# Gates and values of pairs of 512-token blocks by seven products in place of eight, with the weights' combinations formed on the chip and held in DRAM

## The chip, the cores and the metric

The kernel runs on one core of one Trainium2 chip. The metric is the device time of one execution, in microseconds (us), as the median of several runs. The kernel before has a median of 1006.23 us over 3 runs (1005.33 to 1008.88).

## The reference, cut to what matters

Attention on 8 batches of 576 tokens with 8 heads of 64, half of the heads with a local mask of 32 keys and half with a strided one, and then a gated layer on all 4608 tokens:

```python
scores = scale * np.matmul(q, k.transpose(0, 1, 3, 2))
...
attn_out = np.matmul(attn, v)                      # (8, 8, 576, 64)
x = attn_out.transpose(0, 2, 1, 3).reshape(4608, 512)
gate = 1.0 / (1.0 + np.exp(-(x @ w_gate)))         # w_gate: 512 x 1536
val = x @ w_val                                    # w_val:  512 x 1536
out = (gate * val) @ w_out                         # w_out: 1536 x 512
```

The output is 4608 x 512 in float32.

## The kernel before

**Tiling.** The tokens go in nine blocks of 512: block b below 8 holds the first 512 tokens of batch b, and block 8 holds the 64 tokens left over of each batch. The 1536 columns of the gated layer go in 12 slices f of 128. For a slice of a block TensorE forms the gates (`glu_gate`, L371) and the values (`glu_val`, L388), 128 columns by 512 tokens each, in `products` (L364), and a step later adds the slice's share of the output into four PSUM banks (`glu_out`, L416). Each float32 factor is kept as a rounded float32r part h and a rest l, and a product is three matmuls: h by h, h by l and l by h. So the gates of a slice take 4 chunks of the 512 inner columns by 3 matmuls, 12; the values 12; the outputs 4 groups of 128 tokens by 3, 12. A slice is 36 matmuls of 128x128 by 512 columns, a block is 432, and nine blocks are 3888.

**Weights.** The weights come as 64-bit words. In the first stretch of the program they are loaded 512 KB at a time (`load_weight`, W in the order below), turned into float32 by ScalarE (a, b) and VectorE (w), and split into h (u, ScalarE) and l (l, GpSimd). They then stay in SBUF until the end.

**Attention.** A batch has four steps (`pair`, L164), each for two heads: loads (Q, V), scores on TensorE (S), mask, maximum and difference on VectorE (F), exponential on ScalarE (E), sum and division on VectorE (N), a transposition, weighing of the values on TensorE (X), and the split of the result into h (H, ScalarE) and l (L, VectorE), with the left-over tokens set aside (R). The transposition is on TensorE with a copy by ScalarE (T, P) for batches below `BY_PE`, and else in eight pieces on VectorE (B, `turn_blocks`, L254).

**Order.** The first stretch (batches 0 and 1, block 0 and all weights) is written out by hand in `ORDER`, L58, a list of short names that every engine follows. From block 1 on, only TensorE's order is written by hand (L515 to L526): per slice gates, values, outputs of the slice before, and at two of every nine places the next piece of attention(k + 1). A scheduler orders the other engines. DMAs are issued by SyncE (SP), which takes its list in order and waits at an entry until that entry may go.

Of the kernel before, what the change touches and what calls it, by code (L numbers as in the profile page):

```python
# [53 lines left out]

ORDER = """  # L58
C Q00 Q01 W0.0 S00 Z00 F00 S01 a0.0 Q03 W0.1 Q02 b0.0 Z01 F01 E00 W1.0 V01 V00 N00 E01 a0.1 N01 T00 b0.1 W1.1
P00 w0.0 S02 a1.0 b1.0 w0.1 T01 u0.0 W0.2 Z02 F02 u0.1 l0.0 X00 P01 l0.1 a1.1 w1.0 E02 S03 V02 N02 R00 H00  # L60
a0.2 b1.1 L00 T02 b0.2 W2.0 w1.1 u1.0 W2.1 X01 P02 l1.0 Z03 F03 u1.1 g0.0.0 V03 l1.1 Q10 g1.0.0 R01 H01 g0.1.0
w0.2 g1.1.0 E03 L01 a2.1 N03 u0.2 g1.0.1 b2.1 l0.2 X02 a2.0 b2.0 w2.1 W1.2 W2.2 g0.0.1 V10 w2.0 H02 T03 R02
u2.1 L02 g1.1.1 P03 l2.1 g1.0.2 u2.0 a1.2 X03 l2.0 b1.2 W3.0 w1.2 g1.1.2 H03 g0.0.2 R03 L03 u1.2 g0.1.1 a2.2
l1.2 g1.1.3 b2.2 g0.0.3 a3.0 W3.1 w2.2 g0.1.2 s0 g1.0.3 g0.1.3 u2.2 g2.0 b3.0 m0 l2.2 a3.1 W3.2 w3.0 s1 u3.0
b3.1 l3.0 g2.1 x0 W4.0 w3.1 a3.2 y0 u3.1 m1 S10 b3.2 l3.1 x1 W4.1 w3.2 O0 Q11 s2 y1 u3.2 Z10 F10 a4.0 l3.2
b4.0 g3.0 a4.1 W4.2 w4.0 b4.1 E10 W5.0 w4.1 O1 m2 u4.1 N10 x2 l4.1 s3 g3.1 y2 a4.2 u4.0 T10 m3 b4.2 l4.0 g4.1
x3 W5.1 w4.2 P10 y3 a5.0 u4.2 g4.0 b5.0 l4.2 W5.2 w5.0 a5.1 b5.1 u5.0 W6.0 w5.1 X10 s4 l5.0 u5.1 m4 O2 V11
l5.1 a5.2 R10 b5.2 a6.0 W6.1 w5.2 H10 g5.1 b6.0 L10 u5.2 W6.2 w6.0 x4 l5.2 u6.0 y4 O3 a6.1 l6.0 b6.1 W7.0 w6.1
a6.2 g5.0 b6.2 u6.1 W7.1 w6.2 l6.1 u6.2 O4 a7.0 l6.2 s5 b7.0 m5 a7.1 W7.2 w7.0 x5 S11 b7.1 y5 g6.0 u7.0 W8.0
w7.1 Q12 l7.0 Z11 F11 u7.1 a7.2 l7.1 b7.2 g6.1 s6 W8.1 w7.2 a8.0 E11 g7.0 m6 u7.2 N11 x6 l7.2 a8.1 g7.1 s7 y6  # L70
b8.0 T11 m7 b8.1 W8.2 O5 w8.0 P11 W9.0 w8.1 u8.0 l8.0 u8.1 X11 x7 l8.1 a8.2 y7 O6 V12 a9.0 b8.2 b9.0 W9.1 w8.2
R11 g8.0 W9.2 w9.0 u8.2 H11 l8.2 u9.0 L11 g8.1 s8 l9.0 a9.1 b9.1 a9.2 W10.0 w9.1 O7 b9.2 m8 u9.1 W10.1 w9.2 x8
l9.1 y8 u9.2 S12 a10.0 l9.2 b10.0 g9.1 Z12 F12 Q13 W10.2 a10.1 b10.1 W11.0 w10.1 E12 g9.0 w10.0 u10.1 N12
u10.0 l10.1 O8 a10.2 s9 l10.0 T12 b10.2 m9 g10.0 P12 W11.1 w10.2 x9 u10.2 y9 l10.2 X12 s10 a11.0 g10.1 V13 R12
H12 b11.0 L12 W11.2 w11.0 S13 m10 u11.0 O9 Z13 F13 l11.0 x10 a11.1 b11.1 y10 g11.0 E13 w11.1 u11.1 N13 O10 s11
l11.1 a11.2 T13 b11.2 g11.1 P13 w11.2 u11.2 l11.2 X13 m11 x11 R13 y11 H13 L13
# [7 lines left out]
def attention_then_glu(ctx, tc, qk_l, qk_s, v_l, v_s, w_all, consts, out):  # L84
    nc = tc.nc
    pool = ctx.enter_context(tc.tile_pool(name="keep", bufs=1))
    work = ctx.enter_context(tc.tile_pool(name="work", bufs=1))
# [21 lines left out]
    wh, wl = {}, {}

    def stage(n, name):
        return work.tile([P, DM if n[0] in "hl" else 2 * DM], I32, tag=n, name=name)

    def weight_tiles(f):
        wh[f], wl[f] = [None] * 3, [None] * 3
        for i in range(3):
            w = pool.tile([P, 2, DM], F32R, name=f"w{f}_{i}")
            wh[f][i], wl[f][i] = w[:, 0], w[:, 1]

    raws, words = {}, {}  # L120

    order = [(0, 0), (0, 1), (1, 0), (1, 1), (0, 2), (2, 0), (2, 1), (1, 2), (2, 2)]
    order += [(f, i) for f in range(3, NF) for i in range(3)]

    def load_weight(f, i):

        at = order.index((f, i)) % 2
        raws[f, i] = stage(f"raw{at}", f"raw{f}_{i}").rearrange("p (n t) -> p n t", t=2)
        nc.sync.dma_start(raws[f, i], w_all[f, :, i, :, :])

    def upper_words(f, i):
        n = order.index((f, i))
        at = 0 if f == LATE else n % 3
        words[f, i] = stage(f"h{at}", f"high{f}_{i}"), stage(f"l{at}", f"low{f}_{i}")

        to, word = words[f, i][0].bitcast(F32), raws[f, i][:, :, 1].bitcast(F32)
        nc.scalar.activation(to, word, AF.Prelu, scale=2.0**-112, alpha=2.0**32)  # L139

    def lower_words(f, i):
        word = raws.pop((f, i))[:, :, 0].bitcast(U32)
        nc.scalar.activation(words[f, i][1], word, AF.Copy, scale=2.0**-29)  # L143

    def whole(f, i):

        high, low = words[f, i]
        nc.vector.tensor_scalar(high, high, 3, None, op0=ALU.logical_shift_left)
        nc.vector.tensor_tensor(high, high, low, op=ALU.add)  # L149

    def upper(f, i):
        if f == LATE and i == 2:
            w = stage("raw0", f"w{f}_{i}").bitcast(F32R)
            wh[f].append(w[:, :DM]), wl[f].append(w[:, DM:])
        elif f == LATE:
            for ws, t in ((wh, "h"), (wl, "l")):
                ws.setdefault(f, []).append(stage(f"{t}{i + 1}", f"{t}{f}_{i}").bitcast(F32R))
        nc.scalar.copy(wh[f][i], words[f, i][0].bitcast(F32))  # L158

    def lower(f, i):  # L160
        a, _ = words.pop((f, i))
        nc.gpsimd.tensor_tensor(wl[f][i], a.bitcast(F32), wh[f][i].bitcast(F32), op=ALU.subtract)  # L162

    def pair(b, step, space):  # L164
# [5 lines left out]
        nv = (VL if local else SS) * P  # L170
        tiles = {}

        def load_qk(queue=nc.sync):
# [1 line left out]
            queue.dma_start(qk[:, :cols], (qk_l if local else qk_s)[b, p])
# [236 lines left out]
    def glu_out(k, f):  # L416
# [13 lines left out]
        if f < NF - 1:  # L430
            return
# [178 lines left out]
```

## Time and profile before

| | |
|---|---|
| median of 3 runs (lowest, highest) | 1006.23 us (1005.33, 1008.88) |
| the profiled execution: span from the first to the last instruction | 1008.5 us |
| granted TensorE clock in it, mean | 0.998 |
| DMA traffic in it | 66.02 MB |
| HBM read and written | 55.42 MB and 9.44 MB |

The profile gives no time of its own for the execution beside the span, so the span is what a sum is made against. PE is the row of matmuls, PEld that of TensorE's weight loads, DVE is VectorE, ACT ScalarE, POOL GpSimd. Matmuls overlap: the listed duration of one is longer than the distance from one to the next, and the distance is read from merged pieces of the chain of waits ("x12" is twelve matmuls in a row). Idle time of an engine that others do not wait for costs nothing.

### The profile page before, as it was taken

How to read it: one execution, taken by the hardware profiler on the slowest of the kernel's cores; microseconds unless marked ns; L12 is line 12 of the kernel's file. 1: busy time of each engine (PE TensorE's matmuls, PEld its weight loads, DVE VectorE, ACT ScalarE, POOL GpSimd, SP SyncE). 2: the span in 40 equal slices, each digit the busy share in tenths (PEclk: the TensorE clock that was granted, in tenths of full speed). 3: DMA queues.
4: the chain of work that ended last, by engine and by line, in shares of the span. 5: the costliest groups of instructions: out<-in, count | busy, mean ns of one | idle time of the engine just before them, and what ended most of it. 6: DMA issues, size and time to landing. Idle time of an engine off the chain costs nothing.

```text
span 1008.5 us, 18125 instructions
## 1 busy us (share of the span) xinstructions
PE 976.4 (97%) x7840; PEld 793.5 (79%) x7840; DVE 584.4 (58%) x1006; ACT 323.8 (32%) x637; POOL 53.7 (5%) x56
## 2 busy tenths in 40 slices
PE   4899998999999999999999999999999999999997
PEld 3687776888888888888888888888888888888885
DVE  6787766666666566666666666656665733333322
ACT  4787763222322222222222232222222322222221
POOL 1343320000000000000000000000000000000000
PEclk9999999999999999999999999999999999999999
DMA  7665632111211111111111121112110010001001
GB/s 265 210 190 185 202 99 93 40 52 41 83 51 52 41 51 61 49 42 48 71 41 52 41 93 42 52 41 72 62 52 17 1 43 1 0 1 42 1 1 42
DMA packets 19872, 66.02 MB, mean 65 GB/s; under 512 B 2257, under 2 KB 2385, under 8 KB 19793
## 3 DMA queue, kind: packets, MB, share of 16 engines
q1 hardware_dynamic: 18352, 59.28, 18.1%
q10 hardware_dynamic: 1440, 5.59, 1.6%
q8 instruction: 61, 1.00, 0.4%
q14 instruction: 19, 0.15, 0.0%
HBM read 55.42 MB, written 9.44 MB: 64 GB/s over the span
## 4 chain that ended last, share of the span: by engine, by line
PE 85%; DMA 6%; DVE 4%; ACT 4%; issue 0%; SPq 0%; ACTq 0%; DVEq 0%
PE o L423 27%; PE v L369 26%; PE g L369 26%; DMA raw<-in_w_all 5%; PE x L289 3%; PE s L208 2%; ACT high L139 1%; ACT low L143 1%; DVE sb L228 1%; DVE sb L239 0%; DVE high L149 0%; DVE mx L227 0%; DMA qk<-in_qk_l 0%; DVE pt L261 0%; DVE mx L236 0%
## 5 line engine op out<-in xcount | busy, mean ns | idle before, releaser
L423 PE MATMUL o<-w,hh 128*128 128x512 f32 x864 | 270.7, 394 | 1.2 <-DVE ob L436 1.2
L369 PE MATMUL g<-xh,w 128*128 128x512 f32 x784 | 259.3, 391 | 3.8 <-ACT e L378 2.3
L369 PE MATMUL v<-xh,w 128*128 128x512 f32 x784 | 261.4, 394 | 1.1 <-POOL w L162 0.9
L423 PEld LDWEIGHTS o<-w,hh 128*128 128x128 f32 x864 | 159.4, 188 | 36.4 <-issue 2.0
L369 PEld LDWEIGHTS g<-xh,w 128*128 128x128 f32 x784 | 147.4, 188 | 35.6 <-ACT e L378 3.2
L369 PEld LDWEIGHTS v<-xh,w 128*128 128x128 f32 x784 | 147.2, 188 | 34.1 <-POOL w L162 1.4
L423 PE MATMUL o<-w,hl 128*128 128x512 f32 x432 | 168.6, 390 | 0.0
L386 DVE TENSOR_SCALAR t<-t 128x512 int32<-128x512 int32 x96 | 41.0, 427 | 217.9 <-ACT t L383 217.2
L369 PE MATMUL g<-xl,w 128*128 128x512 f32 x392 | 153.0, 390 | 0.4 <-DVE xl L324 0.4
L369 PE MATMUL v<-xl,w 128*128 128x512 f32 x392 | 153.1, 390 | 0.0
L402 ACT ACTIVATE hh<-t 128x512 fp32r<-128x512 f32 x108 | 68.2, 632 | 257.5 <-DVE t L411 255.3
L383 ACT ACTIVATE t<-g 128x512 f32<-128x512 f32 x96 | 57.4, 598 | 267.0 <-PE g L369 262.7
L410 DVE SCALAR_TENSOR_TENSOR e<-e,v 128x512 f32<-128x512 f32 x96 | 65.8, 685 | 91.1 <-PE v L369 91.1
L405 DVE SCALAR_TENSOR_TENSOR hl<-t,hh 128x512 fp32r<-128x512 f32 x108 | 76.7, 710 | 51.1 <-ACT hh L402 51.0
L261 DVE STREAM_TRANSPOSE pt<-sb 32x320 f32<-32x320 f32 (+1 forms) x192 | 103.0, 536 | 3.1
L423 PEld LDWEIGHTS o<-w,hl 128*128 128x128 f32 x432 | 81.1, 188 | 17.9 <-DVE hl L405 0.6
L369 PEld LDWEIGHTS g<-xl,w 128*128 128x128 f32 x392 | 73.7, 188 | 15.8 <-DVE xl L324 0.7
L369 PEld LDWEIGHTS v<-xl,w 128*128 128x128 f32 x392 | 73.6, 188 | 14.4
L411 DVE SCALAR_TENSOR_TENSOR t<-t,e 128x512 f32<-128x512 f32 x96 | 66.5, 692 | 3.2
L384 ACT ACTIVATE e<-g 128x512 f32<-128x512 f32 x96 | 57.0, 594 | 0.0
L162 POOL TENSOR_TENSOR w<-high,w 128x512 fp32r<-128x512 f32 x34 | 46.2, 1369 | 93.6 <-ACT w L158 93.6
L289 PEld LDWEIGHTS x<-pt,vv 64*64 64x64 f32 (+1 forms) x1856 | 34.4, 139 | 12.0 <-issue 10.4
(61 smaller groups left out, 675.6 us busy)
## 6 DMA issues: line engine op xcount, KB each, us to landing
raw<-in_w_all SPq DMA_DIRECT2D x36, 512.0 KB, 4.3
qk<-in_qk_s SPq DMA_DIRECT2D x14, 599.0 KB, 4.1
vv<-in_v_l SPq DMA_DIRECT2D x13, 640.0 KB, 3.9
qk<-in_qk_l SPq DMA_DIRECT2D x14, 592.0 KB, 4.0
out<-ob SPq DMA_DIRECT2D x32, 256.0 KB, 2.0
vv<-in_v_s SPq DMA_DIRECT2D x13, 384.0 KB, 3.0
vv<-in_v_l ACTq DMA_DIRECT2D x3, 640.0 KB, 3.8
qk<-in_qk_s ACTq DMA_DIRECT2D x2, 599.0 KB, 5.2
```

The lines of the kernel that those rows point to most:

```text
L162: nc.gpsimd.tensor_tensor(wl[f][i], a.bitcast(F32), wh[f][i].bitcast(F32), op=ALU.subtract)
L261: nc.vector.transpose(dst[to : to + LB, :, col : col + LB], src[rows : rows + LB, :, h * LB : (h + 1) * LB])
L289: nc.tensor.matmul(xp[j * D : (j + 1) * D, r * BANK + (u * per + g) * m : r * BANK + (u * per + g + 1) * m], v[rows, (u * per + g) * P + j ...
L369: nc.tensor.matmul(o, w, x, start=first and n == 0, stop=last and n == len(todo) - 1)
L383: nc.scalar.activation(t, g, AF.Tanh, scale=0.5)
L384: nc.scalar.activation(e, g, AF.Exp)
L386: nc.vector.tensor_scalar(ti, ti, 0x7FFFFFFF, None, op0=ALU.bitwise_and)
L402: nc.scalar.activation(hh, t, AF.Copy, scale=half)
L405: nc.vector.scalar_tensor_tensor(hl, t, half, hh.bitcast(F32), op0=ALU.mult, op1=ALU.subtract)
L410: nc.vector.scalar_tensor_tensor(e, e, 1.0, v, op0=ALU.min, op1=ALU.mult)
L411: nc.vector.scalar_tensor_tensor(t, t, 1.0, e, op0=ALU.add, op1=ALU.mult)
L423: nc.tensor.matmul(acc[k][i], h[:, i * P : (i + 1) * P], w, start=f == 0 and n == 0, stop=f == NF - 1 and n == 2,)
```

## The change

Blocks 1 to 8 are taken two at a time: (1, 2), (3, 4), (5, 6) and (7, left-over). For such a pair, and for two slices f at a time, gates and values are 2x2 block products: the inner 512 columns in two halves by the two slices, against the same halves by the two blocks. One level of Strassen's scheme (in Winograd's form) forms them from seven products of half the inner length instead of eight: P1 to P7, each 2 chunks by 3 matmuls, for gates and for values. That is 7 x 6 x 2 = 84 matmuls for two slices of two blocks, where there were 4 x 24 = 96.

**The sums.** Seven combinations of x per pair of blocks are formed by VectorE and split by ScalarE and VectorE (`mix_input`, written J in the order; T are the four differences, h and l the splits). Seven combinations of the weights per two slices are formed by GpSimd from the float32 weights and split, 1792 KB for gates and as much for values, once, in the first pair of blocks; they are used from SBUF there, stored in DRAM, and loaded again for the other three pairs (`load_mix`). The sums of products are made in PSUM: ScalarE copies a bank onto another or into SBUF and the next product is added onto it (`pair_of_chunks`). The gate is a Sigmoid on ScalarE, where it was a Tanh and an Exp with three VectorE operations behind them.

**The outputs** of a pair of blocks come after all its gates and values: eight groups of three slices (`group_of_outs`, 36 matmuls each), whose split weights were stored in DRAM in the first stretch and are loaded again for every group, 1536 KB each (`load_outs`). The split of gate times value is made at that load. Loads go into a ring of four tiles w0 to w3, two for each stage, and `load` of a stage is written ahead of the stage before it.

**Elsewhere.** Batch 2 is now in the hand-written order too (`BY_PE` is 3, so it is transposed on TensorE), `ORDER` is new, and the left-over tokens go through DRAM (`rests`). The pieces of attention are placed in the pair stages by a clock that counts products: S at 1, 13, 25 and so on, X at 10.5 after the start, 22.5 and so on.

```diff
-BY_PE = 2
-AT = (0, 7)
-LATE = NF - 1
+BY_PE = 3
...
+PIECE_0, PIECE, PIECE_X = 1, 12, 9.5
+SUPER = ((1, 2), (3, 4), (5, 6), (7, None))
+W_OF = dict(P1=0, P2=1, P4=2, P5=3, P6=4, P7=5, P3=6)
+X_OF = dict(P1=0, P5=1, P2=2, P6=3, P3=4, P7=5, P4=6)
...
+H22 JT1 R22 T23 Jh1 P23 Jl1 X23 H23 JT2 R23 Jh4 JT3 Jh3 Jl4 Jh5 Jl3 Jl5 JT4 Jh6 Jl6
...
+    def keep_rests(b):
+        nc.sync.dma_start(rests[b], rest[b])
...
     def lower(f, i):
...
+        if i == 2:
+            g, n = divmod(f, THREE)
+            nc.sync.dma_start(outer[g][:, n * 2 * DM : (n + 1) * 2 * DM], t.bitcast(F32))
...
+    OBS = ("ob0", "ob1", "ob0", "ob1")
...
+    def next_of_ring(name, n):
+        tag = f"w{ring[0] % 4}"
+        ring[0] += 1
+        return flat(tag, n, name, F32R)
+
+    def load_mix(s, p, i):
+        t = next_of_ring(f"mix{s + 1}_{p}_{i}", 2 * MIX)
+        hold["mix", i, p] = t
+        if s:
+            nc.sync.dma_start(t.bitcast(F32), mixed[p, i])
+            return
...
+        st = flat("st", 4 * PART, f"sums{p}_{i}")
+        s1, s2, s3, s4 = (st[:, n * PART : (n + 1) * PART] for n in range(4))
+        tt = nc.gpsimd.tensor_tensor
+        tt(s1, a21, a22, op=ALU.add)
+        tt(s2, s1, a11, op=ALU.subtract)
+        tt(s3, a11, a21, op=ALU.subtract)
+        tt(s4, a12, s2, op=ALU.subtract)
+        at = 0
+        for src in (a1, a22, st):
+            n = src.shape[1]
+            nc.scalar.copy(t[:, at : at + n], src)
+            tt(t[:, MIX + at : MIX + at + n], src, t[:, at : at + n].bitcast(F32), op=ALU.subtract)
+            at += n
+        nc.sync.dma_start(mixed[p, i], t.bitcast(F32))
...
+        run("P1", g1, v1, lambda: nc.scalar.copy(g2, g1), lambda: nc.scalar.copy(v2, v1))
+        run("P5", g5, v5, lambda: nc.scalar.copy(new("gp"), g5), lambda: nc.scalar.copy(new("vp"), v5))
+        run("P6", g2, v2, lambda: nc.scalar.copy(new("gq"), g2), lambda: nc.scalar.copy(new("vq"), v2), False)
+        run("P2", g1, v1, lambda: sig(new("s11"), g1), lambda: mul(h1[:, :TB], tmp["s11"], v1), False)
...
+        run("P7", g2, v2, *sums("p", "22", g2, v2), False)
+        with tc.high_priority():
+            mul(h2[:, TB:], tmp["s22"], tmp["v22"])
+        run("P3", g5, v5, *sums("q", "12", g5, v5), False)
+        with tc.high_priority():
+            mul(h1[:, TB:], tmp["s12"], tmp["v12"])
+        run("P4", g2, v2, lambda: sig(new("s21"), g2), lambda: mul(h2[:, :TB], tmp["s21"], v2), False)
+
+    def load_outs(s, n):
+        j, g = divmod(n, GROUPS // 2)
...
+        nc.sync.dma_start(hold["o"][-1].bitcast(F32), outer[g])
+        for q in range(THREE):
+            src = hs[g * THREE + q][:, j * TB : (j + 1) * TB]
+            hh, hl = (hold["h"][-1][:, (2 * q + k) * TB : (2 * q + k + 1) * TB] for k in range(2))
+            nc.scalar.copy(hh, src)
+            nc.vector.tensor_tensor(hl, src, hh.bitcast(F32), op=ALU.subtract)
+
+    def group_of_outs(s, n, banks, tick):
+        j, g = divmod(n, GROUPS // 2)
+        (g1, g2, g5), (v1, v2, v5) = banks
+        accs = ([g1, v1, g5, v5], [g1, v1, g2, v2])[j]
...
+        if g == GROUPS // 2 - 1:
+            b = SUPER[s][j]
+            last = s == len(SUPER) - 1 and j
+            with tc.high_priority():
+                store(accs, b, ("ob0", "ob1", "t0", "t1") if last else OBS)
...
+            if k + 1 < len(stages):
+                load(*stages[k + 1])
+            (pair_of_chunks if kind == "p" else group_of_outs)(s, n, banks, tick)
```

**Three places in the order.** The first is VectorE where block 0 ends. Before, ob_1 and ob_3 (two of the four copies of block 0's output) stand among the work on block 1; sb_0 and pt_0 are the first attention step of batch 2, e, t and hl belong to block 1's slices 0 and 1:

```order
L410 SCALAR_TENSOR_TENSOR e_0_1787<-e_0_1787,v_0_1859 128x512
L239 TENSOR_TENSOR sb_0_1799<-sb_0_1799,mx_0_1800 128x640
L411 SCALAR_TENSOR_TENSOR t_0_1788<-t_0_1788,e_0_1787 128x512
L261 STREAM_TRANSPOSE pt_0_1850<-sb_0_1799 32x10x32 x8
L436 COPY ob_1_1893<-o_0_748 128x512
L405 SCALAR_TENSOR_TENSOR hl_0_1873<-t_0_1788,hh_0_1872 128x512
L386 TENSOR_SCALAR t_1_1916<-t_1_1916 128x512
L436 COPY ob_3_1899<-o_1_749 128x512
```

Now the same two copies stand ahead of the last attention step of batch 2 (first_x_103 is its probabilities, s_3 its scores), and the differences and splits of x for the first pair of blocks follow (raw_396 is batch 1, raw_1290 batch 2):

```order
L448 COPY ob_1_1876<-o_0_666 128x512
L448 COPY ob_3_1882<-o_1_667 128x512
L207 TENSOR_TENSOR first_x_103<-s_3_1836,cst 128x6x54 x2
L208 TENSOR_REDUCE first_x_104<-first_x_103 128x12
L209 TENSOR_TENSOR first_x_103<-first_x_103,first_x_104 128x12x54
L217 TENSOR_REDUCE first_x_104<-first_x_103 128x12
L218 TENSOR_SCALAR first_x_104<-first_x_104 128x12
L219 RECIPROCAL first_x_104<-first_x_104 128x12
L220 TENSOR_TENSOR first_x_103<-first_x_103,first_x_104 128x12x54
L342 TENSOR_TENSOR raw_396<-raw_1290,raw_396 128x1024
L354 TENSOR_TENSOR x1l_1982<-raw_396,x1h_1981 128x1024
L342 TENSOR_TENSOR raw_396<-raw_1290,raw_396 128x1024
```

What moved is the whole softmax of batch 2's last step: it is now queued on VectorE behind ob_3, and ob_3 uses the tile of ob_1, whose store must have landed.

The second place is SyncE's list at the end of a block (before: block 1; qk and vv are the next batch's loads):

```order
L175 DMA qk_0_2771<-in_qk_l 128x1184
L179 DMA vv_0_2773<-in_v_l 128x1280
L175 DMA qk_1_3036<-in_qk_s 128x1198
L440 DMA out<-ob_0_2866 128x512
L440 DMA out<-ob_1_2869 128x512
L440 DMA out<-ob_2_2872 128x512
L440 DMA out<-ob_3_2875 128x512
L179 DMA vv_1_3038<-in_v_s 128x768
```

Now, at the end of the first pair of blocks (wo_7 is the last group's output weights, mix_0_0 and mix_0_1 the combinations for gates and values of the next pair's first two slices, mix_1_0 and mix_1_1 those of its second):

```order
L575 DMA wo_7_3937<-outer_79 128x3072
L484 DMA mix_0_0_3981<-mix_0_64 128x3584
L484 DMA mix_0_1_3983<-mix_1_65 128x3584
L452 DMA out<-ob_0_4021 128x512
L484 DMA mix_1_0_4037<-mix_0_66 128x3584
L452 DMA out<-ob_1_4024 128x512
L484 DMA mix_1_1_4039<-mix_1_67 128x3584
L159 DMA qk_1_4245<-in_qk_s 128x1198
L452 DMA out<-ob_2_4027 128x512
L452 DMA out<-ob_3_4030 128x512
```

Each output store now has one or two loads of 1792 KB ahead of it.

The third place is ScalarE there. Before, its list at the end of block 0 holds the copies ob_0 and ob_2 among the gates of block 1:

```order
L384 ACTIVATE e_0_1787<-g_0_1774 128x512
L232 ACTIVATE sb_0_1799<-sb_0_1799 128x640
L438 COPY ob_0_1890<-o_0_748 128x512
L402 ACTIVATE hh_0_1872<-t_0_1788 128x512
L438 COPY ob_2_1896<-o_1_749 128x512
L383 ACTIVATE t_1_1916<-g_1_1902 128x512
```

Now, at the end of the first pair of blocks, ob_2 stands ahead of the exponential of the next attention step and of the copies of P1's banks (o_0 is g1 and g2, o_1 is v1 and v2):

```order
L450 COPY ob_0_4021<-o_0_2063 128x512
L450 COPY ob_2_4027<-o_0_2063 128x512
L213 ACTIVATE sb_0_4049<-sb_0_4049 128x640
L551 COPY o_0_4033<-o_0_4033 128x512
L551 COPY o_1_4034<-o_1_4034 128x512
L552 COPY gp_0_4129<-g_4035 128x512
```

The copies that TensorE's third product (P6) is added onto now come behind two copies for the output.

More of the change, by code (lines that the diff above doesn't have):

```diff
@@ L109, in attention_then_glu @@
[L109 to L164, printed above, removed]
+    mixed = {(p, i): dram.tile([P, 2 * MIX], F32, name=f"mix{p}_{i}") for p in range(PAIRS) for i in range(2)}
+    outer = [dram.tile([P, THREE * 2 * DM], F32, name=f"outer{n}") for n in range(NF // THREE)]
+    rests = [dram.tile([P, NC * REST], F32, name=f"rests{b}") for b in range(B)]
+    xs0 = {}
+    raw = {}
@@ L414, in attention_then_glu @@
[L414 to L434 removed]
+    xs = {}
@@ new lines, in three, with products @@
+    def three(o, pairs, first=True, last=True, onto=False):
+        todo = [m for (wh, wl), (xh, xl) in pairs for m in ((wh, xh), (wh, xl), (wl, xh))]
+        for n, (w, x) in enumerate(todo):
+            nc.tensor.matmul(o, w, x, start=first and n == 0, stop=last and n == len(todo) - 1, skip_group_check=onto)
+    def products(o, f, i, cs=tuple(range(NC)), first=True, last=True):
+        _, h, l = parts_of(f, i)
+        cut = [slice(c * P, (c + 1) * P) for c in cs]
+        three(o, [((h[:, k], l[:, k]), (xs0["h", c], xs0["l", c])) for c, k in zip(cs, cut)], first, last)
@@ L435, in glu_out, with outs, store @@
+    acc = {}
+    def outs(accs, h, w, first, last):
+        hh, hl = h
+        wh, wl = w
+        for i, o in enumerate(accs):
+            for n, (a, b) in enumerate(((hh, wh), (hh, wl), (hl, wh))):
+                nc.tensor.matmul(o, a[:, i * P : (i + 1) * P], b, start=first and n == 0, stop=last and n == 2)
+    def store(accs, b, tags):
+        for i, o in enumerate(accs):
+            ob = flat(tags[i], DM, f"ob{b}_{i}")
             if i % 2:
@@ L460, in attention_then_glu, with first_out @@
-    first_area = ExitStack()
-    first = first_area.enter_context(tc.tile_pool(name="first", bufs=1))
-    x_tiles(0)
-    left_over(0)
-    pairs = {(b, p): pair(b, p, first if b == 0 and p % 2 else work) for b in range(2) for p in range(4)}
+    OBS = ("ob0", "ob1", "ob0", "ob1")
+    def first_out(f):
+        if f == 0:
+            two = [bank(f"o{n}", f"o0_{n}") for n in range(NTT // 2)]
+            acc[0] = [two[i // 2][:, i % 2 * BANK : (i % 2 + 1) * BANK] for i in range(NTT)]
+        _, _, hh, hl = gates(f)
+        _, wh, wl = parts_of(f, 2)
+        outs(acc[0], (hh, hl), (wh, wl), f == 0, f == NF - 1)
+        if f == NF - 1:
+            store(acc.pop(0), 0, OBS)
@@ L465, in attention_then_glu @@
+    first_inputs()
+    pairs = {(b, p): pair(b, p) for b in range(BY_PE) for p in range(4)}
     products_of = {}
-    parts = {}
     def step(what):
```

403 lines of the change are left out of this document (251 added, 152 removed).

## The prediction

> **What bounds the kernel now.** I read the page first, then busy time by stretch, then the chain of waits.
>
> ```profile
> PE 976.4 (97%) x7840; PEld 793.5 (79%) x7840; DVE 584.4 (58%) x1006; ACT 323.8 (32%) x637; POOL 53.7 (5%) x56
> ```
>
> ```profile
> 0.00:160.00 160.00, 136.10 (x1548) 108.15 (x1549) 114.72 (x176) 109.76 (x202) 49.60 (x44) 1.00 0.58 189
> 160.00:1009.00 849.00, 840.26 (x6293) 685.31 (x6291) 469.65 (x830) 214.08 (x436) 4.07 (x12) 1.00 0.13 42
> ```
>
> In the second table the columns after the length are PE, PEld, DVE, ACT and POOL busy, granted clock, DMA share and GB/s. From 160 us on TensorE is busy in 840 of 849 us: nothing but its own work sets the time. In the first 160 us it idles 24 us, and DVE and ACT are busy about 70% there. The chain says what a matmul costs:
>
> ```profile
> 213.05 2.99 PE v L369 x12
> 216.03 2.72 PE o L423 x12
> 218.75 2.72 PE g L369 x12
> ...
> 320.94 2.99 PE v L369 x12
> ...
> 995.87 5.58 PE o L423 x24
> ```
>
> Twelve matmuls take 2.72 us, 0.2267 us each. A block with a batch of attention in it takes 320.94 - 213.05 = 107.9 us, of which 432 matmuls are 97.9, so a batch costs TensorE 10.0 us. TensorE ends at 1001.45, 7 us before the span does; the last copies and stores are unchanged in kind.
>
> **What the change removes.** Each of four pairs of blocks saves 12 of 96 matmuls for six pairs of slices: 72, in all 288 x 0.2267 = 65.3 us. It is all on the path, since TensorE is the path. The output matmuls stay 1728. Attention stays at eight batches, but batch 2 is now transposed on TensorE:
>
> ```profile
> L247 PE MATMUL t<-cst,sb 128*128 128x128 f32 x40 | 7.5, 330 | 9.4 <-DVE sb L239 9.4
> L251 PE MATMUL t<-cst,sb 64*64 64x64 f32 x8 | 1.4, 270 | 0.0
> ```
>
> These are two batches, so a third adds 8.9 / 2 = 4.4 us. The bare sum is 1008.5 - 65.3 + 4.4 = 947.6. What follows is waiting that the old kernel doesn't have.
>
> **Inside a pair stage** (84 matmuls, 19.0 us). A bank that P1, P5 or P6 leaves is copied by ACT while at least 18 matmuls, 4.08 us, run on other banks; the copies and sums are near these rows:
>
> ```profile
> L438 ACT COPY ob<-o 128x512 f32<-128x512 f32 x18 | 10.6, 587 | 26.2 <-PE o L423 14.7 <-DMA out<-ob 11.5
> L436 DVE COPY ob<-o 128x512 f32<-128x512 f32 x18 | 12.4, 688 | 7.3 <-ACT ob L438 3.7 <-DMA out<-ob 3.4
> L378 ACT ACT_TABLE_LOAD x5 | 6.4, 1283 | 0.1
> L162 POOL TENSOR_TENSOR w<-high,w 128x512 fp32r<-128x512 f32 x34 | 46.2, 1369 | 93.6 <-ACT w L158 93.6
> ```
>
> Even behind an exponential (0.74) and two table loads (2 x 1.28) a copy comes in 3.9 us, so I put these at nothing; without that cover each would cost up to 1 us, 24 us over 24 stages. POOL's mixing of two slices, in the first pair of blocks, is 2 x 2816 columns (four sums of 256, splits of 512, 256 and 1024) x 1369/512 ns = 15.1 us, under the 19 us of a stage: hidden. The attention chain has less room. From the end of S to X lie 60 matmuls, 13.6 us. A step before:
>
> ```profile
> 6.82 0.82 DVE L222 TENSOR_TENSOR sb<-s,cst 128x640 f32<-128x640 f32 x1 [6.82 <-PE s L208]
> ...
> 8.53 0.82 DVE L228 TENSOR_TENSOR sb<-sb,mx 128x640 f32<-128x640 f32 x1
> ...
> 10.04 0.73 ACT L232 ACTIVATE sb<-sb 128x640 f32<-128x640 f32 x1
> ...
> 11.82 0.81 DVE L236 TENSOR_REDUCE mx<-sb 128x10 f32<-128x640 f32 x1
> ...
> 13.12 0.82 DVE L239 TENSOR_TENSOR sb<-sb,mx 128x640 f32<-128x640 f32 x1
> ```
>
> ```profile
> L261 DVE STREAM_TRANSPOSE pt<-sb 32x384 f32<-32x384 f32 x96 | 54.7, 570 | 1.5
> ```
>
> F is 2.5 us (6.82 to 9.35), E 0.73 and perhaps 1.28 for a table, N 2.1, eight transposes 4.6: 11.2 us, and up to seven operations of 0.69 for the products stand between them in DVE's order, most in the time of E. I get 12.3 to 14.2 us against 13.6: between nothing and 0.6 us in some of 20 steps, 3 us in all, at most 12.
>
> **The reloads.** Each later stage loads 2 x 1792 KB (gates and values) or 1536 KB (outputs) while the stage before it runs. The nearest rows:
>
> ```profile
> 1.65 0.43 SPq L175 DMA_DIRECT2D qk<-in_qk_s  x1
> 2.12 0.43 SPq L129 DMA_DIRECT2D raw<-in_w_all  x1
> 5.38 1.40 PE L208 MATMUL s<-qk 64*32 64x64 f32 x80 [5.38 <-DMA qk<-in_qk_l]
> ...
> 8.92 0.67 ACT L139 ACTIVATE high<-raw 128x512 f32<-128x512 f32 x1 [6.90 <-DMA raw<-in_w_all]
> ```
>
> ```profile
> 0.00:20.00 20.00, 7.27 (x220) 5.75 (x220) 12.60 (x22) 8.05 (x14) 0.88 (x6) 1.00 0.76 282
> ```
>
> ```profile
> raw<-in_w_all SPq DMA_DIRECT2D x36, 512.0 KB, 4.3
> qk<-in_qk_s SPq DMA_DIRECT2D x14, 599.0 KB, 4.1
> ...
> out<-ob SPq DMA_DIRECT2D x32, 256.0 KB, 2.0
> ```
>
> Loads issued together landed one after another: 599 + 512 KB in 8.92 - 5.38 = 3.54 us, 314 KB/us. The first 20 us moved 282 GB/s at a share of 0.76, which at a full share would be 371 GB/s, 362 KB/us. I take 362 (5.0 us for 1792 KB) with 1.5 us from the last byte to the landing, an estimate from the 2.0 us of a 256 KB store, and keep 314. Two such loads need 11.5 us: hidden in a pair stage. 1536 KB need 5.7 of an output stage's 36 x 0.2267 = 8.2: hidden. But the last output group is only 8.2 us, and ahead of the next pair of blocks it must cover both loads. Count from the end of group seven, 0.5 us to start: gates land at 0.5 + 5.0 + 1.5 = 7.0, values at 12.0. Group eight ends at 8.2, S takes 1.0 and P1's gates 1.4, so P1's values wait 12.0 - 10.6 = 1.4 us. Then the output: ob_3's tile waits for the store of ob_1, which is queued behind three loads and the store of ob_0 (0.5 + 3 x 5.0 + 2 x 0.7 + 1.5 = 18.4); ob_3 takes VectorE 0.7 and frees the bank that ACT's copy of P1's values (0.6) fills for P6. So P6's values start at 19.7 where TensorE comes at 17.4: 2.3. Together 3.7 us, three times: 11. At 314 KB/us it is 6.0, 18 in all; if stores don't queue behind loads and loads are faster, nothing. The left-over tokens come back in seven 128 KB pieces ahead of an output load: 2 us, once.
>
> [...]
>
> **The end of the first stretch.** Here the order makes a serial tail. VectorE's softmax of batch 2's last step is queued behind ob_3, and that behind the landing of ob_1's store; SyncE has a 1792 KB and a 512 KB store ahead of it. Count from the end of block 0's last output matmul: the store of ob_1 lands at 5.5 us (what is left of 5.0 + 1.4, two stores of 0.7, 1.5), ob_3 takes 0.7, F 2.6, E 0.75, N 2.2, the transposition 0.8, its copies with JT1 and Jh1 ahead of them 4, X 0.9: 17.5 us, in which TensorE has 4.9 us of work (transpositions and X of three steps). It idles 12.6. Then P1 and P5 run, but P6's values wait for ACT, which has Jh6 ahead of the copy of P1's values, and that comes behind five operations of VectorE on 1024 columns (some 1.25 us each, from the growth in these two rows):
>
> ```profile
> L360 DVE TENSOR_TENSOR xl<-xr,xh 128x256 fp32r<-128x256 f32 x4 | 1.7, 416 | 0.0
> L324 DVE TENSOR_TENSOR xl<-x,xh 128x512 fp32r<-128x512 f32 x16 | 11.0, 685 | 4.7 <-ACT xh L320 4.7
> ```
>
> ```profile
> 154.65 0.50 PE L369 MATMUL g<-xh,w 128*128 128x512 f32 x1 [1.44 <-ACT xh L320]
> ```
>
> That is 3 to 4 us, in all about 17. The last row, the first gates of block 1, shows that the old seam cost under 2: net 15. If the stores landed alone, in 2.0 us, it would be 12; with ACT late too it is 20.
>
> Before that tail the stretch is denser: for ACT another batch's exponentials (4 x 0.74), copies (4 x 0.9) and the casts of three mixes (3 x 2.1, for 1792 columns at 587/512 ns), 13 us, and twelve stores of 512 KB for SyncE. ACT goes from 70% to nearly 80% there and waits in its order. I add 4 us (0 to 10).
>
> **The clock.** Matmuls behind a stretch of small work and waiting ran slower at first:
>
> ```profile
> 30.12 0.63 PE L369 MATMUL gv<-xh,w 128*128 128x512 f32 x1
> 30.55 0.63 PE L369 MATMUL gv<-xl,w 128*128 128x512 f32 x1
> ...
> 31.57 0.40 PE L369 MATMUL v<-xl,w 128*128 128x512 f32 x1
> 31.81 0.39 PE L369 MATMUL v<-xh,w 128*128 128x512 f32 x1
> ```
>
> They start 0.43 us apart, and 0.24 a microsecond later, although the granted clock's column says 1.00; five or six of them make 1.1 us. I add 1 us for the tail. [...]
>
> **The sum.** 947.6 + 15 (tail) + 11 (three seams) + 3 (attention) + 2 (left-over) + 4 (first stretch) + 1 (clock) = 983.6 us of span. The profiled execution is 2.3 us above the median of the runs shown, so 981.
>
> **The rivals.**
> [...]
> *Reloads bound the later pairs of blocks* (0.08), slower than before. 34.6 MB are reloaded per pair of blocks. Loads that alternate with other traffic took 4.3 us per 512 KB; at that 119 KB/us a group's 1536 KB take 12.9 us against 8.2 and two mixes 30 against about 21.5: 32 x 4.7 + 18 x 8.5 = 300 us more. It decides from about 200 KB/us down: 1536 / 200 + 1.5 = 9.2, 32 x 1.0 us, past 1009. Against it: 314 KB/us where loads did queue.
> *Evacuation waits* (0.12): ACT's order, strict behind table loads and mixing, delays a copy past the 4.08 us in most pair stages; 1 us in each of 24 gives 1005, no change.
> *Fewer matmuls than said, or slower ones*: half the inner length with twice the groups could open gaps between six matmuls; before, groups of 12 follow at 2.72 with no gap, and six-matmul groups have the same pitch if their banks are free. Too weak to price apart.
>
> **The numbers.** My case has 0.6, and its own range is 968 to 996. The measurement tells 0.3%, 3 us. With the rivals the range is 960 to 1003. Faster by over 0.3%: 0.6 + 0.2 and half of evacuation, which has milder forms: 0.86. Same: 0.05. Slower: 0.09.
>
> **What would show it.** Right: 3600 matmuls of 128x512 in place of 3888; PE full inside pair stages; a gap of 10 to 17 us before the first P1 with VectorE waiting for a store of ob; gaps of 2 to 6 us at three places, first on the DMA of mix, then on DVE's ob. Wrong: PE waiting in every output stage for wo (reloads bound), for ACT o in pair stages (evacuation), or X waiting for DVE pt by more than 1 us a step.

## The result and the profile after

The changed kernel takes 1064.84 us (median; 1062.3 to 1066.27), against 1007.48 us of the kernel before on the same chip: a ratio of 1.0557 (95% interval 1.0527 to 1.0588), slower by 5.6%. The forecast was 981. The profiled execution has a span of 1064.1 us, 80.5 above the 983.6 of the sum.

The page of the changed kernel, its head, TensorE's busy time and the granted clock in 40 slices of 26.6 us:

```profile
span 1064.1 us, 17875 instructions
...
PE 953.2 (90%) x7576; PEld 763.5 (72%) x7576; DVE 561.8 (53%) x854; ACT 447.6 (42%) x782; POOL 150.3 (14%) x140
...
PEclk9999987699999999799989998999999989999998
```

TensorE, 97% busy before, is 90% busy now, and its clock, 0.998 before, is granted at 0.953. The 288 matmuls are gone (3600 of 128x512 are left). By stretch (columns as in the prediction: length, PE, PEld, DVE, ACT and POOL busy, clock, DMA share, GB/s; the first row runs to the first product of the pair stages, then pair stages and outputs take turns):

```profile
0.00:204.40 204.40, 155.10 (x2049) 122.17 (x2049) 140.51 (x202) 132.00 (x248) 90.51 (x78) 0.92 0.70 242
204.40:355.20 150.80, 140.69 (x1360) 110.93 (x1357) 108.84 (x169) 83.78 (x142) 58.56 (x56) 0.95 0.43 162
355.20:421.50 66.30, 66.23 (x334) 54.38 (x331) 32.43 (x47) 18.90 (x34) 0.00 (x0) 1.00 0.68 242
421.50:584.30 162.80, 143.72 (x1440) 112.96 (x1438) 98.49 (x165) 68.91 (x117) 0.80 (x4) 0.93 0.49 186
584.30:651.20 66.90, 66.28 (x336) 54.41 (x331) 32.45 (x47) 18.93 (x34) 0.00 (x0) 1.00 0.73 254
651.20:798.40 147.20, 131.65 (x996) 104.97 (x995) 71.43 (x116) 55.55 (x96) 0.40 (x2) 0.95 0.45 174
798.40:864.20 65.80, 65.42 (x288) 53.46 (x287) 25.94 (x34) 17.40 (x28) 0.00 (x0) 1.00 0.62 224
864.20:989.30 125.10, 118.08 (x507) 96.55 (x506) 35.15 (x53) 39.01 (x67) 0.00 (x0) 0.96 0.45 178
989.30:1064.10 74.80, 66.00 (x289) 53.71 (x287) 16.52 (x26) 13.12 (x24) 0.00 (x0) 0.96 0.51 176
```

The outputs run without a gap. The loss is in the first stretch and in the pair stages. A stretch loses in two ways: TensorE is idle (length less busy), or it is busy at half clock (half of its busy time inside the spells that the trace's clock records give 0.5; matmuls of 128x512 that start 0.23 us apart at 297 us start 0.43 apart at 301, inside such a spell). In the changed kernel:

| stretch | idle | lost to half clock | expected in all |
|---|---|---|---|
| to 204.4 us | 49.3 | 10.4 | 44 (24 of it as before) |
| the four runs of pair stages, seams included | 51.8 | 25.2 | 14 |
| outputs and end | 9.9 | 0 | 10 |

What TensorE waits for (total, times, longest):

```profile
PE o L409 <- ACT ob L450: 13.6, 3, 5.2
PE o L409 <- DVE h L538: 13.6, 7, 2.7
...
PE o L409 <- DVE ob L448: 11.9, 3, 4.8
PE o L409 <- ACT s L539: 9.8, 6, 2.0
...
PE o L409 <- ACT gq L553: 2.2, 3, 1.3
```

All five are products on the tiles o_0 and o_1, which hold two banks each, g1 with g2 and v1 with v2; the rows left out between them belong to the first stretch. From 204 us on, products wait 0.7 us in all for the DMA of wo, and no wait for that of mix is listed: the reloads don't bind. What such a wait is, at a P7 of the first pair of blocks (timeline; time, duration, what):

```profile
312.65 1.28 ACT L213 ACT_TABLE_LOAD   x1
...
313.94 0.75 ACT L213 ACTIVATE sb<-sb 128x648 f32<-128x648 f32 x1
...
314.33 0.39 PE L409 MATMUL o<-x2h,mix 128*128 128x512 f32 x1
314.71 1.28 ACT L539 ACT_TABLE_LOAD   x1
...
316.00 0.60 ACT L539 ACTIVATE s<-o 128x512 f32<-128x512 f32 x1
316.65 1.78 PE L409 MATMUL o<-x,mix 128*128 128x512 f32 x6 [1.93 <-ACT s L539]
```

P2 has ended, and the next six matmuls are P7's gates, on g2. They start when the sigmoid of P2's gates ends, and that reads g1, which P7 doesn't touch. The sigmoid is late because an attention step's exponential, with two table loads, stands ahead of it. At the seam between the first two pairs of blocks (chain of waits):

```profile
421.53 0.60 ACT ob L450
...
422.14 5.45 DMA out<-ob
...
427.67 0.04 ACT ob L450
...
428.15 0.75 ACT sb L213
...
431.10 0.50 DVE pt L242
...
435.25 0.70 DVE ob L448
...
435.99 2.93 PE o L409 x6
```

ScalarE stands at ob_2 until the store of ob_0 has landed, 5.45 us; only then comes the exponential of the attention step behind it, then VectorE's softmax and transposes, and behind these ob_3. (The second seam is alike; at the third, which has no attention, ob_3 waits for the store of ob_1 alone, 8.19 us.) P1's gates wait for ob_2, P1's values for ob_3. The two copies read g2 and v2; P1 writes g1 and v1. The clock follows (columns as above):

```profile
420.00:425.00 5.00, 3.10 (x90) 2.31 (x88) 2.49 (x4) 0.59 (x1) 0.00 (x0) 1.00 0.98 408
425.00:430.00 5.00, 1.69 (x4) 1.40 (x5) 1.68 (x4) 1.22 (x2) 0.00 (x0) 0.73 1.03 425
430.00:435.00 5.00, 1.24 (x3) 0.41 (x2) 4.84 (x10) 0.57 (x1) 0.00 (x0) 0.50 0.99 413
435.00:440.00 5.00, 4.01 (x9) 3.14 (x10) 0.91 (x2) 0.57 (x1) 0.20 (x1) 0.50 0.46 176
```

**Theory:** a product waits for whoever last read any bank of its tile, not only its own bank. **Rivals:** VectorE and ScalarE are too slow for the stages whatever the tiles; the reloads crowd the DMA; and, for the first stretch, GpSimd's mixing holds it up.

### The profile page after: what moved, and what is told of

Its sections match the earlier page's. It is cut to its first block, busy times and chain, and to the rows that moved or that the text cites. A ratio compares the mean times of both kernels' runs of the same rounds, so it can differ in the third digit from the quotient of the medians.

```text
span 1064.1 us, 17875 instructions
## 1 busy us (share of the span) xinstructions
PE 953.2 (90%) x7576; PEld 763.5 (72%) x7576; DVE 561.8 (53%) x854; ACT 447.6 (42%) x782; POOL 150.3 (14%) x140
## 4 chain that ended last, share of the span: by engine, by line
PE 61%; DVE 13%; ACT 8%; DMA 8%; issue 7%; POOL 3%; SPq 0%; ACTq 0%; DVEq 0%; POOLq 0%
PE o L409 24%; PE o L442 13%; PE g L409 7%; PE v L409 6%; DVE pt L242 3%; PE g L442 3%; PE v L442 3%; PE x L270 3%; DMA out<-ob 2%; ACT L213 2%; PE s L189 2%; DMA wo<-outer 2%; DMA first_x1l<-in_w_all 1%; POOL mix L500 1%; POOL w L401 1%
## 5 line engine op out<-in xcount | busy, mean ns | idle before, releaser
L442 PE MATMUL o<-wo,hs 128*128 128x512 f32 x864 | 206.5, 390 | 2.1 <-DVE h L538 1.3
L442 PEld LDWEIGHTS o<-wo,hs 128*128 128x128 f32 x864 | 161.3, 188 | 37.9 <-DVE h L538 2.6
L409 PE MATMUL o<-x0h,mix 128*128 128x512 f32 x192 | 74.8, 447 | 36.6 <-ACT ob L450 13.6
L580 DVE TENSOR_TENSOR hs<-h,hs 128x512 fp32r<-128x512 f32 x96 | 61.4, 686 | 84.7 <-ACT hs L579 82.8
L579 ACT CAST hs<-h 128x512 fp32r<-128x512 f32 x96 | 53.2, 620 | 94.6 <-PE o L442 50.7
L409 PE MATMUL o<-x,mix 128*128 128x512 f32 x288 | 76.0, 413 | 12.2 <-DVE h L538 8.0
L409 PEld LDWEIGHTS o<-x0h,mix 128*128 128x128 f32 x192 | 40.7, 212 | 51.8 <-ACT ob L450 14.3
L409 PEld LDWEIGHTS o<-x,mix 128*128 128x128 f32 x288 | 55.5, 196 | 27.5 <-DVE h L538 9.7
L409 PE MATMUL o<-x2h,mix 128*128 128x512 f32 x192 | 64.2, 395 | 2.2 <-ACT gq L553 2.2
L409 PE MATMUL o<-x6h,mix 128*128 128x512 f32 x192 | 63.8, 393 | 0.0
L409 PE MATMUL o<-x3h,mix 128*128 128x512 f32 x192 | 63.5, 392 | 0.0
```

The costliest lines, as they stand in the source:

```text
L409: nc.tensor.matmul(o, w, x, start=first and n == 0, stop=last and n == len(todo) - 1, skip_group_check=onto)
L442: nc.tensor.matmul(o, a[:, i * P : (i + 1) * P], b, start=first and n == 0, stop=last and n == 2)
L579: nc.scalar.copy(hh, src)
L580: nc.vector.tensor_tensor(hl, src, hh.bitcast(F32), op=ALU.subtract)
```

## The experiments

Ratios are to the kernel before on the same chip, with their 95% intervals; the change stands at 1.0557.

**six: a tile for every bank.** The first stretch's PSUM pool is closed ahead of the pair stages and a new one opened:

```diff
-                two = [bank(f"o{m}", f"o{s + 1}_{m}") for m in range(2)]
-                one = [ps.tile([P, BANK], F32, tag=t, name=f"{t}{s + 1}") for t in "gv"]
-                banks = tuple((t[:, :BANK], t[:, BANK:], u) for t, u in zip(two, one))
+                banks = tuple(tuple(ps.tile([P, BANK], F32, tag=f"{t}{n}", name=f"{t}{n}_{s + 1}") for n in (1, 2, 5)) for t in "gv")
```

> The change as it is, but the banks of gates and values of a pair stage are six tiles of one PSUM bank each, in place of two tiles of two banks and two of one; the same products, copies and stores. Theory (a product waits for whoever last read the other bank of its tile): the waits of products inside the pair stages for the sigmoid, for the product of gate and value and for the copy of gq, 9.8 + 13.6 + 2.2 us, mostly go, with about 10 us of half clock behind them; at the three seams the first product no longer waits for the output copies ob_2 and ob_3, though P6 still does, some 4 us each: 1020 to 1035 us. Rival (evacuation itself is too slow, VectorE and ScalarE are behind): the waits move to P6, P7 and P4, less than 10 us gained, 1055 or more. Rival (the reloads hold the pair stages): no change, 1060 to 1066.

Measured: 1004.92 us, 0.994 (0.9917 to 0.9963): 60 us less than the change, and 0.6% below the kernel before. The compiled program shows what the edit does: P2's first product on gates has a wait on ScalarE in the change and none here, since the copy gq reads g2 alone. (Lines of six lie one further down.)

```
change  L409 MATMUL o_0_2063<-x2h_1825,mix_0_0_2037 128x512 [waits Activation_49]
six     L410 MATMUL g_1_2067<-x2h_1825,mix_0_0_2041 128x512
```

The runs of pair stages in six:

```profile
209.00:350.10 141.10, 135.44 (x1365) 109.13 (x1356) 106.26 (x168) 82.96 (x141) 58.68 (x56) 0.98 0.47 173
...
417.60:555.50 137.90, 133.76 (x1367) 107.64 (x1357) 95.82 (x162) 66.02 (x111) 0.80 (x4) 0.99 0.57 215
...
624.60:751.60 127.00, 125.01 (x920) 101.90 (x914) 69.54 (x114) 53.86 (x93) 0.40 (x2) 0.99 0.51 196
...
817.10:934.30 117.20, 114.52 (x506) 94.58 (x505) 34.49 (x52) 38.43 (x66) 0.00 (x0) 1.00 0.48 188
```

They lost 77 us in the change (51.8 + 25.2) and lose 21 here (14.5 idle, 6.7 to the clock). The five waits above are gone; what is left on products:

```profile
PE v L410 <- DVE v L538: 6.0, 2, 3.5
PE v L410 <- DMA mix<-mix: 5.9, 3, 2.7
```

The gain is more than was expected (1020 to 1035): at the seams P6 finds ob_3 done, where 4 us of waiting had been put. The theory is the right one, and the first of its rivals falls, since the same copies and sums on the same engines hardly hold TensorE up (6.0 us behind VectorE's sums).

**obs: four tiles for the output copies.**

```diff
-    OBS = ("ob0", "ob1", "ob0", "ob1")
+    OBS = ("ob0", "ob1", "t8", "t9")
```

> The change as it is, but the four copies of a block's output go to four tiles of their own, so that the third and fourth don't wait for the stores of the first two. Theory (at a seam ScalarE stands at ob_2 until the store of ob_0 has landed, with the exponential of the next attention step behind it, and VectorE's ob_3 stands behind that step's transposes): the waits of products for ob_2 and ob_3, 13.6 + 11.9 us, go to under 5, and most of the 34 us at half clock there, 17 us of loss; the end of the first stretch gets 3 to 6 us shorter: 1018 to 1032 us, and the waits inside the stages stay. Rival (the reloads themselves are late at the seams): the first products wait for the DMA of mix in place of ob, 1050 to 1066.

Measured: 1034.07 us, 1.0233 (1.0215 to 1.0251), 31 us less than the change and 2 above the expected range. The first stretch, which was to get 3 to 6 us shorter, did not: it ends at 205.1 us (204.4 in the change). The waits for ob are gone, those inside the stages are as before (14.2 us on DVE h, 9.8 on ACT s). So the seams' part of the loss needs both: the tile that is shared, and a copy that waits for a store.

**six_obs: both edits.**

> Both edits together: six tiles of one bank, and four tiles for the output copies. Theory: the two add up except at the seams, where either takes part of the same wait: 980 to 1000 us, what is left above the prediction being the end of the first stretch, 20 to 30 us. Rival (the late operations of VectorE and ScalarE only change places): 1030 or more. If the reloads bind: the seams stay at 20 us each.

Measured: 1003.52 us, 0.9933 (0.9909 to 0.9957): nothing beyond six that the measurement can tell. With a tile for every bank the late ob_3 is hidden behind P1 and P5. The expectation of 980 to 1000 was too low; the rest is in the first stretch (below), which loses 48.5 us idle and 14.4 to half clock here.

**half: half the bytes of the mix loads.** The line that sets the load (those that let the products read the rounded part twice are not shown):

```diff
-            nc.sync.dma_start(t.bitcast(F32), mixed[p, i])
+            nc.sync.dma_start(t[:, :MIX].bitcast(F32), mixed[p, i][:, :MIX])
```

> The change as it is, but from the second pair of blocks on only the first half (the rounded parts) of each stored combination of weights is loaded, 896 KB in place of 1792, and the products take the rounded part where they took the rest: the correction by the weights' rest is left out there. Same instructions on all engines, half the bytes of the mix loads. Theory (tile sharing and the order of ob): only the seams get shorter, since a store that stands behind loads of half the size lands 2 to 4 us earlier: 5 to 12 us a run, 1050 to 1060 us. Rival (the reloads bound the later pairs of blocks): 40 us or more gained, and the waits inside the stages of the second and third pair go, while those of the first pair stay.

Measured: 1049.76 us, 1.0385 (1.0357 to 1.0412), 15 us less than the change and near the theory's 1050 to 1060. The waits inside the stages stay (14.1 on DVE h, 9.8 on ACT s); those for ob at the seams fall from 25.5 to 13.7 us. At the first seam the store of ob_0 lands in 4.41 us in place of 5.45, and ob_3 now stands ahead of the step's softmax on VectorE, so what the bytes gave and what the other order gave are not told apart. The stages' waits, which stayed, show that the reloads do not bind; they lengthen the landing that the seam waits for.

**banks: P1's bank shares a tile with P5's in place of P6's.**

```diff
-                banks = tuple((t[:, :BANK], t[:, BANK:], u) for t, u in zip(two, one))
+                banks = tuple((t[:, :BANK], u, t[:, BANK:]) for t, u in zip(two, one))
```

> The change as it is with one line other: the two-bank tiles hold the banks of P1 and P5 (g1 with g5, v1 with v5), and P6's banks g2 and v2 are the tiles of one bank. Theory: a shared tile only costs where the next product on it comes within 6 matmuls (1.36 us) of the copy or sum that reads the other bank; now that is so only for P5 behind P1's copy (0.6 us), all others have 18 matmuls: nearly all of the gain of six tiles, 1005 to 1018 us. Rival (it was not the sharing but what else the six tiles changed in the order of the other engines): 1040 or more.

Measured: 1061.84 us, 1.051 (1.0474 to 1.0546). The expectation of 1005 to 1018 failed, but not in the stages: the runs of pair stages take 534.6 us where they took 585.9. The outputs gave 43 of these 51 us back: 78.5, 78.6, 77.1 and 82.8 us where they took 66.3, 66.9, 65.8 and 74.8. Their waits, and the chain between the two blocks' outputs:

```profile
PE o L442 <- DVE ob L448: 20.4, 4, 5.4
...
PE o L442 <- ACT ob L450: 11.7, 4, 3.0
```

```profile
386.00 7.34 DMA out<-ob
...
393.43 0.70 DVE ob L448
...
394.18 1.65 PE o L442 x3
```

The first block's outputs lie on g1, v1, g5, v5, the second's on g1, v1, g2, v2. Now g5 shares g1's tile, so the second block's first product, on g1, waits for the copy of g5, and that for a store.

**banks_obs: banks, with four tiles for the output copies.** This tests that reading.

> As banks (the two-bank tiles hold P1's and P5's banks), and the four output copies in four tiles of their own, as in obs. In banks the pair stages took 51 us less than in the change, but the four output stretches 12 us more each, because the second block's output starts on g1 and v1 while ob_2 and ob_3, on g5 and v5 in the same tiles, still wait for the stores of ob_0 and ob_1. Theory (sharing of tiles, wherever the two banks are wanted close together): with copies that wait for no store, the two waits between the blocks' outputs shrink from 8 us to under 2, and the time falls to 1010 to 1025 us. Rival (six tiles gained by what else they changed, in the order of the other engines): about what obs alone gave, 1030 or more.

Measured: 1019.2 us, 1.0074 (1.0046 to 1.0102): 43 us below banks. With no store to wait for, the waits between the blocks' outputs are 0.5 us at most (1.5 in all, where they were 32.1). The rival (six gained by something else in the order) falls.

That settles the larger part. The first stretch still ends at 205.4 us in six_obs and 209.1 in six; six kernels go at that. There is one profile of each kernel, and the change, obs and six_obs, with nearly the same first stretch as six, end it at 204.4 to 205.4, so a difference of 4 us here says little. In the names of the order the first digit is the batch, the second the step: S23 are the scores of batch 2's last step.

**warm: matmuls that nothing reads, in the gaps.** In the hand-written order, for instance:

```diff
-... m10 X13 ...
+... m10 D18.v X13 ...
```

> As six_obs, with 70 added matmuls of 128x512 that nothing reads, put in TensorE's order ahead of X13, S23, T22, X21, X22, T23 and X23 (18, 14, 9, 10, 4, 3 and 12 of them, 16 us at full clock), where TensorE stood idle 19 us between 150 and 202 us. Theory (a gap halves the clock of what follows, 14 us of loss in this stretch): the clock stays at 1.00 there, the work between takes 10 to 14 us less, and as the added matmuls partly outlast their gaps 3 to 6 us are given back: 992 to 1000 us. Rival (the half clock doesn't come from the gaps, or the stretch is bound by the other engines and not by TensorE's speed): no gain, 1002 to 1010.

Measured: 1002.36 us, 0.9923 (0.9898 to 0.9948): as six_obs, and above the expected 992 to 1000. The end of the stretch, in six_obs and in warm:

```profile
143.00:205.40 62.40, 41.57 (x672) 33.14 (x665) 38.25 (x44) 34.95 (x73) 42.30 (x34) 0.77 0.67 246
```

```profile
143.00:202.40 59.40, 51.58 (x723) 39.87 (x721) 36.94 (x39) 32.41 (x68) 41.02 (x33) 0.92 0.66 246
```

The clock rises from 0.77 to 0.92, what is lost to half clock there falls from 9.3 to 4.4 us, and the stretch is 3 us shorter. But the added matmuls stood in the way as well: the 14 ahead of S23 run until it starts, at 179.8 us, where it started in six_obs too. So the run does not tell whether the clock is a cause of the late end or only a symptom of the gaps.

**late_mix and late_mix_x: the first mixes behind the last split of the weights,** and in late_mix_x also X21 ahead of S23. `M` forms the sums on GpSimd, `K` does casts and splits:

```diff
-E22 u11.2 N22 T21 l11.2 P21 m11 X20 Jh2 Z23 x11 Jl2 V22 H20 y11 R20 S23 O11 F23 T22 E23 P22 N23 X21 H21 V23 R21 X22
+E22 u11.2 N22 T21 l11.2 M0 P21 m11 X20 Jh2 Z23 x11 Jl2 V22 H20 y11 K0 R20 M1 S23 O11 F23 T22 E23 P22 K1 N23 X21 H21 V23 R21 X22
```

> As six_obs, but the combinations of the weights for the first pair stage are formed behind the last split of the weights (l11.2) on GpSimd, by an entry in the hand-written order, with the sums some entries ahead of the casts, so that ScalarE doesn't stand at a cast until GpSimd has made the sums, nor at x2h (Jh2) until GpSimd has read the tile for l11.2. Theory (GpSimd's mixing, put among its last splits by the scheduler, holds up ScalarE and so the last attention steps of batch 2): the gaps of 4.6 us ahead of X13 and of 3.5 us ahead of S23 go, with most of 10 us at half clock between them: 985 to 997 us. Rival (the end of the first stretch is bound by the shared bank a and the chain of batch 2's last steps): the gaps only move behind, 998 to 1006.

> As late_mix, and in the hand-written order X21, with its copies and the load V23 behind it, stands ahead of the scores S23, and the softmax F23 ahead of the last outputs O11. Theory (X23 waits for V23, whose tile comes free only with X21, and T22 waits in bank a for F23): V23 lands before it is wanted and the gaps ahead of T22 and X23, 2.3 + 2.9 us with their half clock, go: another 5 to 10 us below late_mix. Rival (bank a is used by one step at a time, so any order of the same steps has the same chain): same as late_mix within 3 us.

Measured: 1011.8 us, 1.0025 (1.0003 to 1.0048), and 1008.95 us, 0.9994 (0.9975 to 1.0013): both slower than six_obs, late_mix by 8 us, which neither its theory nor its rival had. In late_mix the gap ahead of X13 goes, but S23 waits 5.3 us in place of 3.5, T23 5.1, and the first product starts at 204.7 where it did at 205.4; the first run of pair stages is then 5.6 us longer. The gaps only moved. late_mix_x starts its pair stages 6 us earlier (199.4) and gives back more, 151 us for the first run of them where six_obs takes 140.

**no_mix: the first pair's combinations are loaded, not formed.**

```diff
-        f = 2 * p
-        a1, a2 = (whole32[n][:, i * DM : (i + 1) * DM] for n in (f, f + 1))
...
+        n = THREE * 2 * DM
+        nc.sync.dma_start(t[:, :n].bitcast(F32), outer[0])
+        nc.sync.dma_start(t[:, n:].bitcast(F32), outer[1][:, : 2 * MIX - n])
```

> As six_obs, but in the first pair of blocks the combinations of the weights are not formed: GpSimd's sums and splits and ScalarE's casts for them are left out, and each tile is filled by loads of as many bytes from the stored output weights; the stores stay, and all later pairs load what was stored, so gates and values are formed from other numbers. Theory (forming the combinations is what holds up the end of the first stretch, by GpSimd's queue and by ScalarE's waits for it): the first product of the pair stages starts 12 to 20 us earlier, 984 to 994 us. Rival (that stretch is set by the last attention steps of batch 2, one behind another, with V23 late): it starts at most 6 us earlier, 996 to 1004; and the first pair's stages, 140 us, hardly change.

Measured: 996.0 us, 0.9859 (0.982 to 0.9898). Its first stretch:

```profile
0.00:203.20 203.20, 157.39 (x2049) 123.12 (x2049) 133.43 (x202) 124.02 (x236) 50.72 (x46) 0.89 0.79 279
```

GpSimd is busy 51 us in place of 90, and the first product comes only 2 us earlier. Another 3.4 us come in the first pair's stages. So forming the combinations is not what holds up the first stretch either, though without it the whole run is 7.5 us shorter than six_obs.

**v23 and tail2: the load V23 into tiles of its own, and the order's end written anew.** In v23, on six (the loads into the two tiles, and V23's place in the order, are not shown):

```diff
+            if (b, step) == (2, 3):
+                tiles["v"] = v = flat("t8", TB, "vv2_3"), flat("t9", TB, "vv2_3b")
```

In tail2, on v23:

```diff
+S22 a11.2 y10 b11.2 w11.2 u11.2 l11.2 M0 O10 F22 s11 g11.1 E22
+N22 T21 P21 m11 X20 Jh2 x11 Jl2 V22 H20 y11 R20 X21 H21 R21 Z23 S23 F23 O11 T22 E23 P22 N23 K0 M1 X22
```

> As six, but the values of batch 2's last step (V23) are loaded into two tiles of their own, ahead of the scores S22, in place of the tile that X21 frees. Theory: X23 no longer waits for a load issued at 193 us that took 8.6 us to land; X23 then follows the turned probabilities 2 to 4 us earlier: 1000 to 1004 us. Rival (the split of the combinations on GpSimd is still later): no change, 1003 to 1008.

> As v23, with the end of the hand-written order written anew: the last weights' split (w11.2, u11.2, l11.2) ahead of the softmax F22, X21 ahead of the scores S23, F23 ahead of the last outputs, and the combinations for the first pair stage with sums well ahead of casts, the casts behind P22 and P23. Theory (the end of the first stretch is a chain of waits between engines in hand-set order, none of them long): the first product of the pair stages starts 8 to 15 us earlier than with six, and half of the clock's loss there goes: 985 to 998 us. Rival (it is GpSimd's work itself that sets the end): no change, 1003 to 1010.

Measured: 1006.45 us, 0.9964 (0.9946 to 0.9983), no change from six although its pair stages start at 203.0 us; and 1001.78 us, 0.9915 (0.9889 to 0.9941), above its expected 985 to 998 but the lowest median of the kernels that compute all of the reference, though its interval overlaps those of six, six_obs and warm. In tail2 the pair stages start at 197.8 us, 11 earlier than in six, and their first run takes 146.4 us where six takes 141.1: part of the waiting went from one side to the other.

So what sets the end of the first stretch is not settled. GpSimd's mixing, V23 and single places in the order were each changed alone, and none moved the end by more than some 6 us; the new order moved it by 11 and gave half of that back. By the end of the first run of pair stages the kernels are close again: 345.5 us in six_obs, 344.2 in tail2, 345.2 in v23, 350.1 in six, 350.3 in late_mix and 350.8 in late_mix_x; only no_mix is earlier, 339.8. What is left is the chain of batch 2's last steps through five engines in hand-set order, with the half clock behind its gaps; that was only argued.

## Why the prediction was wrong, step by step

**Work removed: right.** Busy time at full clock is 953.2 - 35.6 = 917.6 us, where the sum had 976.4 - 65.3 + 4.4 = 915.5. One figure of the prediction is wrong without effect on the sum: the output matmuls are 9 x 12 x 12 = 1296, not 1728.

**Inside a pair stage: wrong, and this is the step that failed.** "A bank that P1, P5 or P6 leaves is copied by ACT while at least 18 matmuls, 4.08 us, run on other banks" counts to the next product on the same bank. The program waits per tile, and on the same tile the next product follows after six matmuls, 1.36 us: P2 behind the copy gq, P7 behind the sigmoid and the product of P2, P1 behind those of P4. The step's own rows would have shown it as too little: two table loads and an exponential ahead of a copy, 3.9 us by its own count, don't fit into 1.36. Outside the seams the pair stages lost 26.3 us idle and 14.1 to half clock, where the sum had 3 (for attention); 25.6 us of the idle time are the waits on h, s and gq shown above. The rival "evacuation waits" had the right kind of wait, but priced it at 1 us a stage and 24 in all, with no clock and no seams. With a tile for every bank, in six, the four runs of pair stages lose 21 us with their seams, of 77.

**The seams: the links right, their end wrong.** The store of ob_0 or ob_1 behind the loads, the copy behind the store and the product behind the copy are all in the trace. Two links were missed: ob_2 holds up ScalarE's exponential, and ob_3 stands (at the first two seams) behind that step's softmax and transposes; and the shared tile makes P1 wait in P6's place. In the 24, 21 and 16 us behind the three seams TensorE is idle 25.5 us and loses 11.1 to half clock, where 11 were forecast. In six, P1's values wait 5.9 us in all for the loads of mix, where 3 x 1.4 = 4.2 were forecast, and P6 not at all where 3 x 2.3 were.

**The DMA's rate.** From 420 to 435 us, at a share of 0.98 to 1.03, the seam moved 408 to 425 GB/s, above the 371 that was worked out from the first 20 us; the 5 us before moved 370 at 0.98. Yet the seams did not go to nothing: six still waits 2 us at each. The 960 us at the lower end of the range and the chance of 0.2 stand for seams at no cost, through loads at a higher rate, and no run shows that term: in six, six_obs and banks_obs products wait 5.9, 5.6 and 5.7 us in all for the loads of mix.

**The clock: mis-sized most.** 1 us was added, 35.6 were lost, 25.2 in the pair stages. The 1 us was worked out from five or six slow matmuls behind one stretch of small work; what was missing were the gaps in the pair stages, 51.8 us of idle time, and the half clock behind them.

**The first stretch: size.** Expected 20 us of loss over the kernel before, measured 49.3 + 10.4 - 23.9 = 35.8. The forecast long wait, VectorE ahead of ob_3, was short (2.9 us, ended by ScalarE's ob_2, which waited 3.05 for the store of ob_0): the stores of 1792 and 512 KB that were put ahead of it had been issued at 173.8 and 175.0 us, 7 us before the first copy was ready. In its place stand seven gaps of 1 to 5 us, and the half clock.

**Attention, left-over tokens, reloads, end:** as expected or less. X waits 0.7 us for VectorE's transposes, the outputs run full, and no load of wo delays a group by more than 0.5 us.

In sum: 983.6 + 63 (pair stages and seams) + 16 (first stretch) + 2 (work) = 1064.6, against 1064.1.
